# Linear attention and a gated feed-forward block: how the reciprocals of the denominators reach the rows of q

## The chip, the cores and the metric

One Trainium2 chip, one of its cores. The metric is the device time of one execution in microseconds (us); of several executions the median is given. The engines are PE (matrix products, with its weight loads as PEld), DVE, ACT and POOL (elementwise work), and SP, which here only issues transfers. Each runs its own queue in order; sixteen DMA engines move the data.

## The reference

The input x has 2048 rows of 576. It is normalised row by row (xn). Two branches read xn:

```python
qkv = xn @ wqkv                      # 32 heads of 18
phi = lambda t: where(t > 0, t + 1, exp(t)) + 1e-6
pq, pk = phi(q), phi(k)
kv  = einsum("hsd,hse->hde", pk, v)  # one 18 x 18 matrix a head
z   = einsum("hsd->hd", pk)
num = einsum("hqd,hde->hqe", pq, kv)
den = einsum("hqd,hd->hq", pq, z) + 1e-6
s   = (num / den).reshape(S, D) @ wo
g   = silu((gelu(xn @ w_gate) * (xn @ w_up)) @ w_down)
out = x + s * g
```

The change concerns the division by den: one number for each head and each row of x.

## The kernel before, in words

**Layout.** The 2048 rows of x are four blocks of 512 (tb 0 to 3), each of four tiles of 128 (t). Most products run in float32r, each operand cut into a rounded part and a rest (`split`, L101; `halve`, L700), so that a product is a few passes. Products written in plain float32 show as two instructions each in the trace. Nearly every instruction is pinned to the order in which the program writes it (`act`, `vec`, `mm`, `pool`, `dma`, L86 to L99), so the order on each engine's queue is the order of the text; all of these helpers' instructions carry the helper's line (PE L93, DVE L90, ACT L87, POOL L96, transfers L99), and the trace's groups are told apart by tiles.

**The order of the work.** First k and v for the 16 tiles, one `kv_tile` (L475) a tile: three products `x_mm` (c = 0, 1, 2; the third also gives 64 columns of q), the elementwise `k_post`, `v_post`, `q_parts`, `q_post`, and `kv_mm` (L366), which adds to the matrices kv of all heads; the operands of the next tile are made by `place` and `norm`, whose statistics come from `x_next` (L1213, `bn_stats` on DVE). After tile 7 come q's products for blocks 0 and 1 (`q_store`, L512, whose result goes to DRAM), after tile 15 those for blocks 2 and 3 (`q_hold`, L517, whose result stays in SBUF). Between these stand lists of other work, written out by hand (`behind`, `aside`). Then s for all blocks (`s_mm`, L720; 28 products a tile), then 36 matrices of the gate and up products and the down products, which are most of the time and which the diff doesn't touch.

**q.** phi(q) lies with q's columns on the partitions and the rows of x along the free dimension, in five groups (gi): four of seven heads (126 partitions, and on the last two partitions two of the columns of the last head, so that these four are full), and a fifth of four heads (72 columns; `q_turn`, L457, transposes it and two rows for each of the four groups out of the third product of a tile). `phi` (L355) is: a minimum with zero, on ACT (`Relu` of -q) for odd blocks and on DVE for even ones; a maximum on DVE; exp on ACT; an add on POOL.

**kv times wo.** `kv_done` (L562) masks kv's sums into kvm. `kv_wo(gi)` (L588) multiplies a group of kvm by its rows of wo and cuts the result into kvh and kvl, the operands of s. One more column of wo, which is 1 in row 0 only, gives z, the sum of phi(k), as the last column of the second product of each group. From z DVE makes `zc`, z placed in a column a head with the mask `maskh` (part of the tile named small in the trace). `move_rows` (L626) copies the rows of the last head to the last two partitions of the four groups, zc's by way of zx (in the tile named eps_t).

**The division before.** `den(tb)` (L671) multiplies zc by phi(q): 20 small products into one bank, quarters of the block on quarters of the partitions, so that the 32 heads' denominators of 512 rows stand as 128 x 128. DVE adds 1e-6 and takes the reciprocal (tile r); ACT and DVE lay r out as the operand rd (tile aux), rounded part and rest. `scale(tb, gi)` (L692) multiplies `sel`, a matrix of ones and zeros, by rd on PE (tile b, 128 x 512), which repeats each head's reciprocal on that head's 18 partitions, and DVE multiplies phi(q) by it. `halve` then makes the operands of s (tile pq). `make_sel` and `copy_sel` build sel on POOL and ACT. The blocks of s come in the order 2, 3, 0, 1; blocks 0 and 1 of phi(q) are loaded back from DRAM by SP (`q_load`, L526) while s of the blocks before runs.

**Space.** PSUM has six shared banks (`bank`) and two of another ring (`own_bank`). The SBUF slots that matter here are b7 and b8 (a block of phi(q) each; b7 held a fifth of the weights of k and v before), b15 (aux before) and b12 and b14 (wo and kvm, later the operands pq of every second block).

Of the kernel before, what the change touches and what calls it, by code (L numbers as in the profile page):

```python
# [55 lines left out]
def block_kernel(ctx, tc, x, xe, xt_d, wq_d, wkv0_d, wkv1_d, wkv2_d, wo, wgu_d, wd_d, out):  # L56
# [330 lines left out]
    pkv, pks, vas, es, pqt, ph4, ph, ph_d = ({} for _ in range(8))  # L387
# [69 lines left out]
    def q_turn(t):  # L457
# [5 lines left out]
        if i == 0:  # L463
            ph4[tb] = gl_tile([P, TBN], f"ph4_{tb}")
            if tb < 2:
                ph_d[tb] = dr.tile([P, NHG, TBN], F32, name=f"phd_{tb}")
        act(ph4[tb][:, i * P : (i + 2) * P], b[:, 0:P2], AF.Copy)
        if i == 2 and tb < 2:
            dma(out=ph_d[tb][:, 4, :], in_=ph4[tb])
# [5 lines left out]
    def kv_tile(t, early=(), middle=(), end=(), after=()):  # L475
# [7 lines left out]
        if t % 2 == 0 and t % (2 * TT):  # L483
            q_turn(t - 2)
# [5 lines left out]
        run(list(middle))  # L490
        if t - 1 in vas:
            kv_mm(t - 1)
# [6 lines left out]
    def q_mm(tb, gi, o):  # L499
# [10 lines left out]
        phi(o, pq, f"q{tb}_{gi}", tb % 2 == 1)  # L510

    def q_store(tb, gi):  # L512
        o = gl_tile([P, TBN], f"ph_{tb}_{gi}")
        q_mm(tb, gi, o)
        dma(out=ph_d[tb][:, gi, :], in_=o)

# [6 lines left out]
    def ph_of(tb, gi):  # L523
        return ph4[tb] if gi == 4 and tb > 1 else ph[tb][:, gi, :]
# [17 lines left out]
    def make_masks():  # L542
# [15 lines left out]
        band(at["maskh"], ones.rearrange("p (g h) -> p g h", g=NHG), [[-GW, NHG], [DH, H]], 1)  # L558
# [14 lines left out]
    def load_wo():  # L573

        n = NHG * P
        t = big(14, [P, 2 * n + D + 2], F32, "kvm")
        at["one"] = t[0:H, n + D + 2 :].rearrange("p (g j) -> p g j", g=NHG)
        at["kvm"] = t[:, 0:n].rearrange("p (g j) -> p g j", g=NHG)
        at["wo"] = w = big(12, [P, 4, D + 2], F32, "wo_t")
        at["wo4"] = w4 = t[:, n : n + D + 2]  # L580
# [5 lines left out]
        dma(out=w4[1 : W4 + 1, 0:D], in_=wo[4 * GW : D, :])  # L586

    def kv_wo(gi):  # L588
# [8 lines left out]
        zc, mh = at["zc"], at["maskh"]  # L597
# [3 lines left out]
        for c, cs in enumerate((slice(0, HALF), slice(HALF, D + 2))):  # L601
            pw.append(bank(f"kw_{gi}_{c}"))
            mm(
                pw[c][0:wdt, 0 : cs.stop - cs.start], at["kvm"][0:k, gi, 0:wdt], w[0:k, cs],
# [3 lines left out]
        z = pw[1][:, HALF : HALF + 1]  # L608
# [6 lines left out]
        if gi == 4:  # L615
            vec("tensor_copy", zx[x_], z[x_])
# [3 lines left out]
        vec("tensor_scalar", zc[r, gi, :], mh[r, gi, :], z[r], None, op0=ALU.mult)  # L620
# [5 lines left out]
    def move_rows():  # L626
        for gi in range(4):
            r, e = slice(Q4 + 2 * gi, Q4 + 2 * gi + 2), slice(GW, P)
            dma(out=at["zc"][e, gi, H - 1 : H], in_=zx[r])
# [3 lines left out]
    def make_sel():  # L633

        n = NHG * P
        buf = big(15, [P, n + TBN], F32R, "aux")
        at["sel"] = sel = buf[:, 0:n].rearrange("p (g j) -> p g j", g=NHG)
        at["rd"] = rd = buf[:, n : n + TBN]
        one = at["one"]
        pool("memset", one, 1.0)  # L640
        four, last = one[:, 0:4, 0:GW], one[:, 4, :].rearrange("p (r j) -> p r j", r=2)
        for o, pattern, base in ((four, [[GW, 4], [1, GW]], 0), (last, [[0, 2], [1, Q4]], 4 * GW)):
            pool(
                "affine_select",
                out=o, in_=o, compare_op=ALU.is_ge, fill=0.0, base=base,
                pattern=pattern, channel_multiplier=-DH,
            )
            pool(
                "affine_select",
                out=o, in_=o, compare_op=ALU.is_ge, fill=0.0, base=DH - 1 - base,  # L650
                pattern=[[-s_, n_] for s_, n_ in pattern], channel_multiplier=DH,
            )
        pool(
                "affine_select",
            out=one[:, 0:4, GW:P], in_=one[:, 0:4, GW:P], compare_op=ALU.is_ge, fill=0.0,
            base=1 - H, pattern=[[0, 4], [0, P - GW]], channel_multiplier=1,
        )
        pool("memset", rd.bitcast(F32), 0.0)

    def copy_sel():  # L660
        one, sel = at["one"], at["sel"]
        for i in range(4):
            r = slice(i * H, (i + 1) * H)
            if i % 2:
                act(sel[r], one, AF.Copy)
            else:
                pool("tensor_copy", sel[r], one)

    HB = TBN // 4

    def den(tb):  # L671

        pd = bank(f"d_{tb}")
        for gi in range(NHG):
            for i in range(4):
                mm(
                    pd[H * i : H * (i + 1), 0:HB], at["zc"][:, gi, :],
                    ph_of(tb, gi)[:, i * HB : (i + 1) * HB],
                    start=(gi == 0), stop=(gi == NHG - 1),
                )  # L680
        r = gl_tile([P, HB], f"r_{tb}")
        rd = at["rd"]
        vec("tensor_scalar", r, pd[:, 0:HB], EPS, None, op0=ALU.add)
        vec("reciprocal", r, r)
        for i in range(4):
            c, rows, low = slice(i * HB, (i + 1) * HB), slice(H * i, H * (i + 1)), i ^ 1
            act(rd[rows, c], r[rows], AF.Copy)
            vec("tensor_sub", rd[H * low : H * (low + 1), c], r[rows], rd[rows, c].bitcast(F32))

    pqs, s_d, words = {}, {}, {}  # L690

# [743 lines left out]
```

## Time and profile before

| | |
|---|---|
| median of 3 runs | 1492.97 us (1492.86 to 1493.04) |
| the profiled execution | 1492.91 us |
| its span, first to last instruction | 1491.2 us |
| PE / DVE / ACT / POOL busy | 99% / 71% / 38% / 36% of the span |
| granted clock of PE | 1.000 |
| q's products of blocks 2 and 3, with kv times wo | about 183 to 217 us of the span |
| s | about 217 to 286 us |

The times in a row of the trace start at the first instruction of the span. The span is 1.7 us shorter than the execution's own time. A row of the order of time has start, duration, engine, line, operation, output and inputs, shape, count, and in brackets how long the engine was idle before it and who ended that. A row of a group has busy time and mean duration behind the first bar, and the idle time before its instructions with its enders behind the second. A row of a stage lists the busy time of PE, PEld, DVE, ACT and POOL, the granted clock, the share of the DMA engines and their rate.

### The profile page before, as it was taken

What the parts mean: (1) busy time and instruction counts of PE and PEld (TensorE: products, weight loads), DVE (VectorE), ACT (ScalarE), POOL (GpSimd) and SP (SyncE); (2) the same over time, 40 slices, a digit from 0 to 9 for tenths busy, and PEclk for the clock granted to TensorE, in tenths of its full rate; (3) what the DMA queues carried; (4) which work ended last, traced back from release to release, by engine and by line L of the source; (5) the groups of instructions that cost most, each with busy time, mean ns of one, the idle gap of its engine ahead of it and who ended that gap; (6) DMA issues with size and microseconds to landing.
All of it is one profiled execution on the core that took longest, in us unless ns stands there. A gap on an engine that the chain in (4) does not pass through costs nothing.

```text
span 1491.2 us, 22334 instructions
## 1 busy us (share of the span) xinstructions
PE 1481.9 (99%) x8355; PEld 1327.8 (89%) x8355; DVE 1063.9 (71%) x1586; ACT 560.9 (38%) x1043; POOL 543.6 (36%) x521
## 2 busy tenths in 40 slices
PE   9999999999999999999999999999999999999998
PEld 8989989988888888888888888888899999999998
DVE  7667577377788787788787778787785575555775
ACT  5535445332232232332222322223445454445443
POOL 5442431144665544565554565554310020001120
PEclk9999999999999999999999999999999999999999
DMA  6355015533443423444433344333697766686873
GB/s 238 131 213 180 1 43 194 206 149 132 165 173 144 162 106 132 149 174 152 157 119 122 143 173 171 138 134 119 216 335 252 235 215 220 226 292 217 299 253 113
DMA packets 114614, 260.67 MB, mean 175 GB/s; under 512 B 10234, under 2 KB 38778, under 8 KB 112458
## 3 DMA queue, kind: packets, MB, share of 16 engines
q1 hardware_dynamic: 112730, 249.95, 46.7%
q0 software_dynamic: 1632, 8.91, 1.6%
q8 instruction: 65, 1.06, 0.3%
q10 hardware_dynamic: 144, 0.39, 0.1%
q14 instruction: 43, 0.35, 0.1%
HBM read 161.27 MB, written 97.91 MB: 174 GB/s over the span
## 4 chain that ended last, share of the span: by engine, by line
PE 94%; DVE 2%; DMA 2%; ACT 1%; issue 0%; POOL 0%; SPq 0%; ACTq 0%; DVEq 0%; POOLq 0%
PE bd L1010 27%; PE al L804 15%; PE ga L804 15%; PE de L804 15%; PE be L804 8%; PE kv L93 6%; PE s L93 4%; PE q L93 2%; DMA kept_T<-xo_T 1%; PE kv_a L93 1%; ACT xo_T L87 0%; DMA xf_B<-in_xt_dram 0%; PE d L93 0%; PE kw L93 0%; DVE xo_T L90 0%
## 5 line engine op out<-in xcount | busy, mean ns | idle before, releaser
L1010 PEld LDWEIGHTS bd<-t,s 128*128 128x128 f32 x3024 | 400.9, 188 | 0.1
L1010 PE MATMUL bd<-t,s 128*128 128x288 f32 x3024 | 401.0, 295 | 0.0
L90 DVE TENSOR_TENSOR s<-sr,s 128x512 fp32r<-128x512 f32 x252 | 176.1, 739 | 119.8 <-ACT s L87 117.8
L87 ACT ACTIVATE s<-sr 128x512 fp32r<-128x512 f32 x252 | 149.1, 626 | 189.0 <-PE bd L1010 131.0
L96 POOL TENSOR_TENSOR hs<-h,h 128x512 f32<-128x512 f32 x68 | 94.7, 1401 | 203.8 <-DVE h L90 201.1
L87 ACT ACTIVATE h<-h 128x512 f32<-128x512 f32 x108 | 67.1, 633 | 244.5 <-POOL sm L96 123.1
L96 POOL TENSOR_TENSOR sx<-sx 128x288 f32<-128x288 f32 x24 | 27.9, 1180 | 322.9 <-DVE sx L90 321.8
L93 PE MATMUL kv<-wkv,xo_B 128*128 128x416 f32 (+1 forms) x672 | 129.9, 349 | 0.0
L93 PEld LDWEIGHTS kv<-wkv,xo_B 128*128 128x128 f32 x672 | 121.4, 188 | 1.3 <-POOL wkv L96 0.2
L90 DVE TENSOR_TENSOR wa<-raw,wa 128x256 fp32r<-128x256 f32 x72 | 79.2, 1100 | 50.8 <-ACT wa L87 47.5
L96 POOL TENSOR_TENSOR sm<-raw 128x384 f32<-128x384 f32 x72 | 75.8, 1053 | 107.1 <-DMA raw<-in_wgu_dram 86.5
L90 DVE TENSOR_TENSOR h<-h,u 128x512 f32<-128x512 f32 x108 | 95.7, 886 | 3.7
L87 ACT ACTIVATE wa<-sm 128x1152 fp32r<-128x1152 f32 x36 | 41.8, 1161 | 135.8 <-PE de L804 135.8
L90 DVE TENSOR_TENSOR wa<-sm,wa 128x768 fp32r<-128x768 f32 x72 | 63.1, 877 | 36.9 <-ACT wa L87 36.1
L96 POOL TENSOR_TENSOR td<-td 128x288 f32<-128x288 f32 x72 | 70.1, 973 | 53.0 <-DMA td<-in_wd_dram 48.7
L90 DVE TENSOR_TENSOR wb<-raw,wb 128x256 fp32r<-128x256 f32 (+1 forms) x108 | 72.0, 666 | 7.3 <-ACT wb L87 5.8
L90 DVE TENSOR_TENSOR wb<-sm,wb 128x256 fp32r<-128x256 f32 x72 | 61.3, 852 | 20.6 <-ACT wb L87 20.0
L87 ACT ACTIVATE u<-al 128x512 f32<-128x512 f32 x72 | 40.9, 592 | 88.4 <-PE al L804 88.4
L90 DVE TENSOR_TENSOR u<-u,ga 128x512 f32<-128x512 f32 x72 | 49.3, 686 | 19.9 <-PE ga L804 19.3
L804 PE MATMUL al<-xo_B,wa 128*128 128x512 f32 x252 | 63.0, 389 | 0.0
L804 PE MATMUL be<-xo_T,wa 128*128 128x512 f32 x252 | 63.0, 389 | 0.0
L804 PE MATMUL be<-xr_T,wa 128*128 128x512 f32 x252 | 63.0, 389 | 0.0
(175 smaller groups left out, 2773.4 us busy)
## 6 DMA issues: line engine op xcount, KB each, us to landing
sr<-hs SPq DMA_DIRECT2D x252, 256.0 KB
hs<-h SPq DMA_DIRECT2D x68, 512.0 KB
raw<-in_wgu_dram SPq DMA_DIRECT2D x36, 768.0 KB
hs<-hs SPq DMA_DIRECT2D x102, 256.0 KB
td<-in_wd_dram SPq DMA_DIRECT2D x18, 576.0 KB
td<-td SPq DMA_DIRECT2D x18, 576.0 KB
tr<-td SPq DMA_DIRECT2D x16, 576.0 KB
tr<-in_wd_dram SPq DMA_DIRECT2D x12, 576.0 KB
```

The source lines that it names most:

```text
L87: pin(nc.scalar.activation(*args, **kw))
L90: pin(getattr(nc.vector, op)(*args, **kw))
L93: pin(nc.tensor.matmul(*args, **kw))
L96: pin(getattr(nc.gpsimd, op)(*args, **kw))
L804: nc.tensor.matmul(o, w[0:rows, wi, :], xop[0:rows, xi, :], start=(start and n == 0), stop=(n == len(PASSES) - 1), skip_group_check=True,)
L1010: nc.tensor.matmul(banks[j][:, 0:HALF], hw[n, s][:, a, t * P : (t + 1) * P], w[:, c, g % 4], start=(new and g == 0 and m == 0), stop=(g == ...
```

## The change

The products with sel go, with sel, rd and their making. The reciprocals r (32 heads by 512 rows) are written to DRAM (`rd`) by a transfer from POOL's queue, and `to_rows` reads them back by six transfers from POOL's queue into `rb`, which holds for each of q's 128 partitions and five groups the reciprocal of its head. `scale` is now one DVE product of phi(q) and rb, both in SBUF. The first of the six carries four groups. The heads have other numbers inside zc and den: the head in place i of the full group g has the number 4 i + g, and `make_masks` builds maskh accordingly.

- z comes from products of its own, `key_sums`, ahead of `kv_wo`, with the copies to zx and zc and the four small transfers for zc's last rows, which were in `kv_wo` and `move_rows`. kv_wo's second product has 288 columns instead of 290.
- The blocks of s come in the order 0, 2, 3, 1. Block 0 is loaded from DRAM ahead of q's products of block 2; block 3 is stored to DRAM and loaded back. Block 3's denominators are summed in three pieces between other work, by `den_mm`, from the tiles that are stored.
- `phi` takes its minimum on ACT for all blocks.
- `q_turn` stands behind the third product of its tile, and not behind the second.
- `x_next` for tiles 10, 12 and 14 stands earlier in the lists.

```diff
-    def phi(o, src, name, even):
+    def phi(o, src, name):
         e = tmp(list(o.shape), f"e_{name}")
-        if even:
-            act(e, src, AF.Relu, scale=-1.0)
-        else:
-            vec("tensor_scalar", e, src, 0.0, None, op0=ALU.min)
+        act(e, src, AF.Relu, scale=-1.0)
         vec("tensor_scalar", o, src, 0.0, EPS, op0=ALU.max, op1=ALU.add)
-        act(e, e, AF.Exp, scale=-1.0 if even else 1.0)
+        act(e, e, AF.Exp, scale=-1.0)
         pool("tensor_add", o, o, e)
...
         x_mm(t, 1)
-        if t % 2 == 0 and t % (2 * TT):
-            q_turn(t - 2)
...
         x_mm(t, 2)
         run(list(middle))
+        if t % 2 == 0 and t % (2 * TT):
+            q_turn(t - 2)
...
+    def key_sums():
+        pz = bank("z")
+        zc, mh = at["zc"], at["maskh"]
+        for gi in range(NHG):
+            wdt, k = (W4, W4 + 1) if gi == 4 else (GW, GW + 1)
+            w = at["wo4"] if gi == 4 else at["wo"][:, gi]
+            mm(
+                pz[0:wdt, 2 * gi : 2 * gi + 2], at["kvm"][0:k, gi, 0:wdt], w[0:k, D : D + 2],
+                start=True, stop=True,
+            )
+        x_ = slice(Q4, W4)
+        vec("tensor_copy", zx[x_], pz[x_, 8:9])
+        for gi in range(NHG):
+            r = slice(0, Q4 if gi == 4 else GW)
+            z = pz[r, 2 * gi : 2 * gi + 1]
+            vec("tensor_scalar", zc[r, gi, :], mh[r, gi, :], z, None, op0=ALU.mult)
+        for gi in range(4):
+            dma(out=zc[GW:P, gi, H - 1 : H], in_=zx[Q4 + 2 * gi : Q4 + 2 * gi + 2])
...
-    def make_sel():
...
-    def copy_sel():
...
+    def den_mm(tb, gi, src, first, last):
+        if first:
+            dens[tb] = own_bank(f"d_{tb}")
+        for i in range(4):
+            mm(
+                dens[tb][H * i : H * (i + 1), 0:HB], at["zc"][:, gi, :],
+                src[:, i * HB : (i + 1) * HB], start=first, stop=last, skip_group_check=True,
+            )
+
+    def den_end(tb):
+        r = gl_tile([P, HB], f"r_{tb}")
+        vec("tensor_scalar", r, dens[tb][:, 0:HB], EPS, None, op0=ALU.add)
+        vec("reciprocal", r, r)
+        rd[tb] = dr.tile([H, TBN], F32, name=f"rd_{tb}")
+        dma(out=rd[tb].rearrange("h (i c) -> i h c", i=4), in_=r, eng=nc.gpsimd)
...
+    def to_rows(tb):
+        rb[tb] = o = big(15, [P, NHG, TBN], F32, f"rb_{tb}")
+        four = rd[tb][0 : 4 * HG].rearrange("(i g) c -> i (g c)", g=4)
+        dma(
+            out=o[0:GW, 0:4, :].rearrange("p g c -> p (g c)"),
+            in_=four[:, None, :].to_broadcast([HG, DH, 4 * TBN]), eng=nc.gpsimd,
         )
+        last = rd[tb][H - 1 : H, None, :]
+        dma(out=o[GW:P, 0:4, :], in_=last.to_broadcast([2, 4, TBN]), eng=nc.gpsimd)
+        for r in (0, Q4):
+            for h, n, k in ((4 * HG, 3, DH), (H - 1, 1, Q4 - 3 * DH)):
+                src = rd[tb][h : h + n, None, :].to_broadcast([n, k, TBN])
+                dma(out=o[r : r + n * k, 4, :], in_=src, eng=nc.gpsimd)
+                r += n * k
...
     def scale(tb, *gs):
         for gi in gs:
-            pb = bank(f"b_{tb}_{gi}")
-            mm(pb, at["sel"][:, gi, :], at["rd"], start=True, stop=True)
             p = ph_of(tb, gi)
-            vec("tensor_mul", p, p, pb)
+            vec("tensor_mul", p, p, rb[tb][:, gi, :])
...
-    q_hold(2, 7, [
-        [lambda: kv_mm(2 * N0 - 1), kv_done, lambda: difference(1, 3)],
-        [lambda: q_turn(2 * N0 - 2), lambda: kv_wo(4)],
-        [lambda: kv_wo(0), lambda: kv_wo(1), move_rows],
-        [lambda: kv_wo(2), lambda: kv_wo(3)],
+    q_load(0, 7)
+    q_hold(2, 8, [
+        [lambda: kv_mm(2 * N0 - 1), kv_done],
+        [key_sums, lambda: q_turn(2 * N0 - 2), lambda: difference(1, 3)],
+        [lambda: den(0), lambda: to_rows(0), lambda: kv_wo(4)],
+        [move_rows, lambda: kv_wo(0), lambda: kv_wo(1)],
     ])
-    q_hold(3, 8, [
-        [lambda: den(2)],
-        [lambda: scale(2, 0, 1), lambda: halve(2, 0, 1)],
-        [lambda: scale(2, 2, 3), lambda: halve(2, 2, 3)],
-        [lambda: scale(2, 4), lambda: halve(2, 4)],
-    ])
+    behind = [
+        [lambda: kv_wo(2), lambda: scale(0, 0, 1), lambda: halve(0, 0, 1)],
+        [lambda: kv_wo(3), lambda: den(2), lambda: scale(0, 2, 3), lambda: halve(0, 2, 3),
+         lambda: den_mm(3, 4, ph4[3], True, False), lambda: den_mm(3, 0, pg[0], False, False)],
+        [lambda: scale(0, 4), lambda: to_rows(2), lambda: halve(0, 4),
+         lambda: den_mm(3, 1, pg[1], False, False)],
+        [lambda: q_load(3, 7)],
+    ]
+    for gi in range(4):
+        q_store(3, gi)
+        run(behind[gi])
...
     aside = {
...
+        (0, 0): [lambda: den_mm(3, 2, pg[2], False, False), lambda: den_mm(3, 3, pg[3], False, True), lambda: den_end(3),
+                 lambda: build(1, "T1", X_SLOT["T1"])],
+        (0, 1): [lambda: scale(2, *five), lambda: halve(2, *five), lambda: to_rows(3),
+                 lambda: q_load(1, 8)],
+        (0, 3): [lambda: build(1, "T3", X_SLOT["T3"]), lambda: load_mat(0)],
+        (2, 0): [lambda: scale(3, *five), lambda: halve(3, *five), lambda: back("B11")],
+        (2, 1): [lambda: build(1, "T2", X_SLOT["T2"]), lambda: den(1), lambda: to_rows(1)],
+        (2, 3): [lambda: build(1, "T4", X_SLOT["T4"]), lambda: back("T2")],
+        (3, 0): [lambda: mat_sums(0)],
+        (3, 1): [lambda: scale(1, *five), lambda: halve(1, *five)],
+        (3, 3): [lambda: back("T1")],
...
-    for tb in (2, 3, 0, 1):
+    for tb in S_ORDER:
```

More of the change, by code (lines that the diff above doesn't have):

```diff
@@ L386, in block_kernel @@
     left = {}
-    pkv, pks, vas, es, pqt, ph4, ph, ph_d = ({} for _ in range(8))
+    pkv, pks, vas, es, pqt, ph4, ph, ph_d, pg = ({} for _ in range(9))
     def x_mm(t, c, passes=None, new=bank):
@@ L509, in q_mm @@
                 n += 1
-        phi(o, pq, f"q{tb}_{gi}", tb % 2 == 1)
+        phi(o, pq, f"q{tb}_{gi}")
     def q_store(tb, gi):
@@ L523, in ph_of @@
     def ph_of(tb, gi):
-        return ph4[tb] if gi == 4 and tb > 1 else ph[tb][:, gi, :]
+        return ph4[tb] if gi == 4 and tb == 2 else ph[tb][:, gi, :]
     def q_load(tb, i):
@@ L660, in copy_sel @@
-    def copy_sel():
[L661 to L688, printed above, removed]
+    HB = TBN // 4
@@ new lines, in den @@
+    def den(tb):
+        for gi in range(NHG):
+            den_mm(tb, gi, ph_of(tb, gi), gi == 0, gi == NHG - 1)
+        den_end(tb)
+    def to_rows(tb):
[4 more added lines that the diff above has]
+            in_=four[:, None, :].to_broadcast([HG, DH, 4 * TBN]), eng=nc.gpsimd,
+        )
+        last = rd[tb][H - 1 : H, None, :]
[5 more added lines that the diff above has]
+                r += n * k
```

83 lines of the change are left out of this document (25 added, 58 removed).

## The prediction, made before the change was run

> **What bounds the kernel now.** I read the page first (busy shares, slices, chain), then the waits of PE, then a table by stage, then the order of time in the stages that change.
>
> ```profile
> span 1491.2 us, 22334 instructions
> PE 1481.9 (99%) x8355; PEld 1327.8 (89%) x8355; DVE 1063.9 (71%) x1586; ACT 560.9 (38%) x1043; POOL 543.6 (36%) x521
> PEclk9999999999999999999999999999999999999999
> PE 94%; DVE 2%; DMA 2%; ACT 1%; issue 0%; POOL 0%; SPq 0%; ACTq 0%; DVEq 0%; POOLq 0%
> ```
>
> PE works for all but 9.3 us of the span at the full granted clock, and 94% of the chain is PE. So a product that goes saves its own time, unless something else comes late in the place that it leaves.
>
> ```profile
> PE qx L462 <- POOL w_q L96: 1.1, 1, 1.1
> PE b L93 <- DVE aux L90: 0.2, 1, 0.2
> ```
> ```profile
> 183.00:217.40 34.40, 34.40 (x193) 27.80 (x192) 27.25 (x50) 16.71 (x36) 14.41 (x12) 1.00 0.01 3
> 217.40:285.60 68.20, 67.98 (x586) 65.71 (x585) 39.24 (x64) 32.19 (x66) 7.49 (x9) 1.00 0.47 174
> ```
>
> Two of PE's few waits lie in what the diff touches. In the two stages of the change (q's blocks 2 and 3, then s) the columns are PE, PEld, DVE, ACT and POOL: PE has no gap, DVE is 79% and 58% busy, POOL 42% and 11%, and the DMA engines are idle in the first stage. There is room beside PE, but a queue in order can still be late.
>
> **What goes from PE.** The twenty products b (five a block).
>
> ```profile
> 226.10 0.69 PE L93 MATMUL s<-kv,pq 128*128 128x288 f32 x4
> 226.63 0.63 PE L93 MATMUL b<-aux 128*128 128x512 f32 x2
> 227.10 0.42 PE L93 MATMUL s<-kvh,pq 128*128 128x288 f32 x2
> ...
> 230.82 0.85 PE L93 MATMUL b<-aux 128*128 128x512 f32 x3
> 231.51 0.42 PE L93 MATMUL s<-kvh,pq 128*128 128x288 f32 x2
> ```
>
> From start to start two take 0.47 us and three 0.69: 1.16 a block, 4.64 in all. With the wait of 0.2 above: **-4.8 us**.
>
> The turn of q's last columns moves behind the third product of its tile (x_mm(t, 2)).
>
> ```profile
> 132.90 0.27 PE L462 MATMUL qx<-ident,w_q 128*128 128x128 f32 x1
> 134.22 0.33 PE L462 MATMUL qx<-ident,w_q 128*128 128x128 f32 x1 [1.05 <-POOL w_q L96]
> 134.31 2.72 PE L93 MATMUL kv<-wkv,xo_B 128*128 128x384 f32 x14
> ```
>
> The wait of 1.05 us for POOL falls inside the 2.6 us of those 14 products: **-1.05**. DVE's shift of x_next by a tile leaves the operands of tile 10 as late as now, with over a microsecond to spare by my count; I cost that at nothing (0 to +1 if the spare is gone).
>
> **What comes to PE.** key_sums: five products in fp32 with two columns, ten instructions in the trace's counting (all fp32 products show twice). None such is shown; the nearest rows:
>
> ```profile
> 186.37 1.04 PE L93 MATMUL kv_a<-pk,va 128*127 128x126 f32 x8
> 187.25 0.29 PE L93 MATMUL kv_b<-pk,va 128*73 128x72 f32 x2
> 187.35 1.41 PE L93 MATMUL q<-xo_B,wq 128*128 128x512 f32 x5
> ```
>
> 0.11 us an instruction with 126 columns, 0.05 with 72: 0.5 to 1.1 us, I take **+0.8**. The sums of denominators (160 instructions) stay, but block 3's are cut into three groups, and a return from fp32 to the other form costs.
>
> ```profile
> 239.12 1.23 PE d L93 x40
> 240.35 3.91 PE s L93 x28
> 244.26 0.47 PE b L93 x2
> 244.73 3.72 PE s L93 x28
> ```
>
> 28 products take 3.91 us behind d and 3.72 behind b. I count seven fp32 groups before and eight after, since kw and den now share some: **+0.2**. So PE's own work and known waits: -4.85.
>
> **What now waits.** T is microseconds from q's first product of block 2 (183.06 in before). With 3.3 for 14 products of q, 1.0 for kv_mm, 0.9 for a kv_wo, 1.3 for a den, PE reaches den(0) at T 12.0, s of block 0 at 36.6, the last denominators of block 3 at 40.8.
>
> *First wait: den(0) on the two rows that SP copies into zc.*
>
> ```profile
> 192.64 0.16 DVE L90 COPY eps_t<-kw 8x1 f32<-8x1 f32 x1
> ```
> ```profile
> 192.83 0.71 SPq L99 DMA_DIRECT2D small<-eps_t  x1
> 193.70 0.62 SPq L99 DMA_DIRECT2D kvh<-kv  x1
> 194.41 0.56 SPq L99 DMA_DIRECT2D kvl<-kv  x1
> ```
> ```profile
> GB/s 0 0 0 0 0 0 0 0 0 0 0 18 0 0 18 0 0 0 0 18 0 18 0 0 0 0 18 0 0 18 0 33 0 0 0 18 0 0 18 0
> ```
>
> Before, den came 5 us behind these transfers. Now DVE copies the sums when phi's max of q's second product is done, T 9.3; SP issues four transfers 0.6 apart from there (0.03 after the copy, as above). The last row is the DMA rate from 192 to 202 in quarters: the 4.5 KB of kvh, issued at 193.70, move at 194.75. Landing at 1.1 (these bytes) to 3.5 us (the shortest landing listed, 512 KB below); I take 1.7: they land at T 11.0 to 12.9, and the group that needs the last is multiplied at 12.9. **+0.3** (0 to 2). Behind it stands PE's whole queue.
>
> *Second wait: POOL.* It issues the write of the reciprocals, waits until that has landed, issues six transfers, and only then does what stands behind.
>
> ```profile
> 215.35 1.30 POOL L96 TENSOR_TENSOR ph<-ph,e_q 128x512 f32<-128x512 f32 x1 [2.35 <-DVE ph L90]
> ```
> ```profile
> 1090.15 1.08 POOL L99 DMA_DIRECT2D hs<-hs  x2
> ```
> ```profile
> 239.99 0.70 POOL L99 DMA_DIRECT2D xr_B<-kept_B  x1 [19.72 <-ACT s L87]
> ```
> ```profile
> xr_T<-kept_T POOLq DMA_DIRECT2D x3, 1280.0 KB, 7.2
> hs<-h POOLq DMA_DIRECT2D x4, 512.0 KB, 3.5
> xr_B<-kept_B POOLq DMA_DIRECT2D x1, 1280.0 KB, 9.3
> ```
>
> An issue is 0.54 us (0.70 at most), so six are 3.2, and 1280 KB, just what the rows of a block weigh, land in 7.2 to 9.3 us. A broadcast from DRAM is not in the trace; I take 7.2, its own smaller rows included. Block 0: den ends at T 13.6, reciprocal (0.95) and sum 15.0, write landed 18.1, rows landed 25.3. DVE wants them behind phi and kv_wo(2), at 25.5: just hidden. Behind the waiting POOL stand the memset for kv4 and phi's add for q's fourth product; den(2) needs that one only at 27.9, and it is done by 24.
>
> Block 2 is the tight one. DVE's queue from 25.5 holds, without a gap, scale and halve of block 0, phi's max of three products and the second reciprocal:
>
> ```profile
> 214.51 0.69 DVE L90 TENSOR_SCALAR ph<-q 128x512 f32<-128x512 f32 x1 [0.24 <-ACT e_q L87]
> 215.12 1.28 DVE L90 TENSOR_TENSOR ph<-ph,b 128x512 f32<-128x512 f32 x2
> 216.50 1.30 DVE L90 TENSOR_TENSOR pq<-ph,pq 128x512 fp32r<-128x512 f32 x2
> ```
>
> At 0.6 to 0.7 each it frees rb at T 35.5. POOL then issues six (3.2) and adds q's last phi (1.3): 40.0 to 41. PE needs that add at 40.8: **+0.5** (0 to 2).
>
> A row shows how the add can be longer:
>
> ```profile
> 174.70 0.72 POOL L96 TENSOR_TENSOR w_q<-w_q 128x64 f32<-128x64 f32 x2 [0.80 <-ACT w_q L87]
> ...
> 183.48 3.52 POOL L96 TENSOR_TENSOR w_q<-w_q 128x64 f32<-128x64 f32 x2 [1.07 <-ACT w_q L87]
> ```
> ```profile
> 183.27 3.55 DVE L90 TENSOR_TENSOR xf_B<-xf_B,xf_B 128x1536 f32<-128x1536 f32 x2
> ```
>
> The same two adds took 3.52 us instead of 0.72 beside a DVE operation with both inputs in SBUF. Scale's second factor now lies in SBUF, so this can happen beside it too; one such product is 0.6 us and is inside the bound of 2. The Trainium skill ("SBUF — State Buffer", Who interferes with whom) says the same, that such an operation and a GpSimd read lock each other out for a whole instruction; by it the second wait would be nearer 1.1 than 0.5, and the trace agrees with the lock.
>
> *The rest is hidden.* Blocks 2, 3 and 1 have 12, 16 and 11 us from POOL's first issue to the first s that needs them, against 7.2 and some 4 us of DVE. SP's loads of q's blocks wait for their slots and hold the stores of s behind them; tmp has four buffers for those. What DVE and ACT no longer do (four subtractions and copies a den, DVE's min for even blocks) is off the path.
>
> **Sum.** -4.8 - 1.05 + 0.8 + 0.2 + 0.3 + 0.5 = -4.05 from the profiled execution's 1492.91 us (span 1491.2 and 1.7 around it), which is 0.06 under the median 1492.97: **1488.9 us**.
>
> **Rivals.**
>
> *The stalls eat the gain.* With issues of 0.70 (six: +1.0), rows in 9.3 us (block 0 lands at 27.4, 1.9 later than DVE wants, and DVE's gapless queue hands that on to rb and to the last add), and key_sums at 1.1, the sum is +3 more: 1491.9, no difference that shows. For it: POOL's queue and DVE's are in order and have under a microsecond to spare. Against: 0.54 and 7.2 are the usual rows.
>
> *Slower: rows from DRAM come much later than a plain load.* The place is scale of block 0. From a landing of some 8 us after the first issue each microsecond more is one of PE's at the last denominators of block 3, and from 12 block 2 adds as much again, since s of block 2 starts at T 53 and POOL's issue for it at 36. At 16 us the cost is 8 + 4: 1501. It decides from about 14 on (8 - 2 make up the 4 gained and 3 above). For it: 18 rows read the same 8 KB each, in a shape no row shows. Against: nothing else uses the DMA engines in the first stage (3 GB/s), and 1280 KB in 16 us would be 80 GB/s where the loads shown make 140 to 180.
>
> The Trainium skill ("DMA: Bandwidth & Descriptors", Rules for kernel authors) has a rule against the change: an outermost dimension under 16 confines a transfer to that many engines. The broadcast's source goes out as 7 regions, and seven sixteenths of that page's 341 GB/s make an estimate of 6.9 us for the moving of the big transfer, so a landing near 8.5 and a sum near 1490. No run here shows it yet.
>
> *The change does not do what it says:* the products go but PE is held elsewhere by as much. With no gap in PE and room on DVE I see no such place beyond the two waits above; it is within the first rival.
>
> **Chances.** A measurement of this kernel tells 0.2%, 3.0 us, from no change. My forecast with its bounds (1486.9 to 1490.2): 0.62; better still: 0.04; first rival, to 1493: 0.20; slower by transfers: 0.14. That makes faster 0.68 (a fifth of the first rival and most of the forecast), same 0.17, slower 0.15. The range 1486.9 to 1493.0 leaves out the last case and the better one.
>
> **What would show it.** Right: no b on PE; the wait of qx gone; PE's waits name small's transfer before the first d, and ph's add by POOL before the third group of block 3's d, each under a microsecond; the rows land about 7 us behind the issue. Wrong: PE waiting on DVE for pq at the start of s, six issues of POOL far above 3.2 us, a DVE wait on rb, or a wait that moves to the first gate products. The sum is wrong if key_sums takes more than 1.1 us or PE's pitch changes beside the transfers.

## The result: 18 us slower

The changed kernel takes 1511.09 us (median; 1507.97 to 1512.7) where the kernel before takes 1492.97: ratio **1.0118**, 95% interval 1.0103 to 1.0133. The forecast was 1488.9. The profiled execution took 1509.51 us, with a span of 1507.8, so 16.6 us more span than before. Of the executions behind the ratios in this text two took far longer than the rest (5462.67 us of e9, 2649.49 us of the kernel before) and are left out of the ratios.

The page of the changed kernel: span, busy shares, granted clock in 40 slices, and the chain.

```profile
span 1507.8 us, 22351 instructions
PE 1483.9 (98%) x8345; PEld 1328.6 (88%) x8345; DVE 1055.3 (70%) x1562; ACT 558.4 (37%) x1033; POOL 560.2 (37%) x549
PEclk9999998999999999999999999999999999999999
PE 89%; DVE 3%; DMA 3%; issue 3%; POOL 1%; ACT 1%; SPq 0%; POOLq 0%; ACTq 0%; DVEq 0%
```

PE is busy 2 us more than before although the products b are gone, the chain's PE share fell from 94% to 89%, and the clock row shows an 8 in the seventh slice (226 to 264 us), which the row of before doesn't have. So the loss has a place. PE's waits name it (microseconds in all, times, longest):

```profile
PE d L93 <- DMA ph<-phd: 9.4, 1, 9.4
PE s L93 <- ACT pq L87: 2.9, 1, 2.9
PE d L93 <- POOL ph L96: 2.4, 1, 2.4
...
PE s L93 <- DVE pq L90: 1.0, 1, 1.0
```

Four new waits, 15.8 us. The largest is den(1), the denominators of block 1, waiting for SP's load of that block (ph from phd). The next one in size is the first s of block 1, waiting for pq, which waits for rows (the 1.0 belongs to it); the third is the last denominators of block 3, waiting for POOL's add of phi. None stands at scale of block 0.

The same waits in order of time, PE's rows:

```profile
226.34 0.43 PE L93 MATMUL d<-ph,small 128*32 128x128 f32 x8 [2.44 <-POOL ph L96]
...
255.05 2.36 PE L93 MATMUL d<-ph,small 128*32 128x128 f32 x40 [9.44 <-DMA ph<-phd]
...
261.82 0.42 PE L93 MATMUL s<-kvh,pq 128*128 128x288 f32 x2
...
283.56 0.85 PE L93 MATMUL s<-kvh,pq 128*128 128x288 f32 x2 [2.92 <-ACT pq L87]
...
285.91 1.33 PE L93 MATMUL s<-kvh,pq 128*128 128x288 f32 x4 [1.02 <-DVE pq L90]
...
290.83 0.42 PE L93 MATMUL s<-kvh,pq 128*128 128x288 f32 x2
...
294.56 0.42 PE L93 MATMUL s<-kvh,pq 128*128 128x288 f32 x2
```

The forty products d behind the long wait take 2.36 us, against 1.23 in the prediction's row of before. A table by stretches says why; the column behind the five engines is the granted clock.

```profile
250.00:255.00 5.00, 0.00 (x0) 0.00 (x0) 0.00 (x0) 0.00 (x0) 0.00 (x0) 0.50 1.01 276
255.00:259.00 4.00, 3.95 (x47) 3.60 (x48) 2.17 (x4) 1.45 (x3) 0.00 (x0) 0.52 0.77 278
259.00:263.00 4.00, 4.00 (x32) 4.00 (x31) 2.58 (x5) 2.52 (x6) 0.00 (x0) 1.00 0.34 140
283.50:289.80 6.30, 5.22 (x21) 4.87 (x22) 4.85 (x8) 3.62 (x9) 0.57 (x1) 0.52 0.32 126
```

**A long wait of PE is paid twice.** The clock falls to 0.50 while PE stands idle, and stays at about 0.5 for the next 4 to 6 us. The tile of s behind den(1) is done 6.77 us after that den began (255.05 to 261.82), where the prediction's rows of before have 5.14 from 239.12 to 244.26: 1.6 us. The first tile of block 1 takes 7.27 us (283.56 to 290.83) and the next 3.73 (to 294.56); take off the wait of 1.02 and 2.5 remain. So 15.8 of waits and 4.1 of half clock, less the gain of 3.6 that the first experiment below measures, make 16.3 of the 16.6 us.

What holds the load? First the rows of reciprocals alone, block 0, 200 to 212 us: the DMA engines' busy share in forty slices (tenths), what was moved, and landing times from the issue.

```profile
DMA  1010000670544545757888765764663499510001
...
DMA packets 919, 1.66 MB, mean 138 GB/s; under 512 B 566, under 2 KB 566, under 8 KB 790
...
rb<-rd POOLq DMA_DIRECT2D x1, 1008.0 KB, 9.9
```

Though almost nothing else is moving, the share is 0.4 to 0.8, not 0.9, and the transfer needs 9.9 us; the prediction took 7.2 from a plain load. Then the stretch of the long wait, 232 to 260 us, in which block 3's rows, the loads of q's blocks and the transfer of B11 back meet:

```profile
DMA packets 2024, 7.17 MB, mean 256 GB/s; under 512 B 701, under 2 KB 701, under 8 KB 1548
...
xr_B<-kept_B POOLq DMA_DIRECT2D x1, 1280.0 KB, 20.9
rb<-rd POOLq DMA_DIRECT2D x1, 1008.0 KB, 19.8
```

What POOL's queue has in flight takes about 20 us. Block 1's load is issued into that:

```profile
233.54 0.32 SPq L99 DMA_DIRECT2D ph<-phd  x1
...
238.84 0.32 SPq L99 DMA_DIRECT2D ph<-phd  x1
```

The second of these is block 1's, and den(1) begins at 255.05: 16.2 us from the issue. PE had come to it at 245.61 (255.05 less 9.44), 6.8 us from the issue. In the kernel before the same pair stands far apart. Block 1 is the last block of s in both orders, but den(1) stood behind the first tile of the third block, and now stands behind the second tile of the second, so that its rows have time to come:

```profile
236.99 0.40 SPq L99 DMA_DIRECT2D ph<-phd  x1
```
```profile
256.52 1.30 PE L93 MATMUL d<-ph,small 128*32 128x128 f32 x40
```

That is 19.5 us, more than the 16.2 here and the 18.6 that e2 shows below. The change takes 12.7 us of this cover away and puts new transfers into what is left. DVE waits for rows in the same way, for the first block little, for blocks 3 and 1 long:

```profile
211.17 1.29 DVE L90 TENSOR_TENSOR ph<-ph,rb 128x512 f32<-128x512 f32 x2 [2.84 <-DMA rb<-rd]
...
256.83 2.50 DVE L90 TENSOR_TENSOR ph<-ph,rb 128x512 f32<-128x512 f32 x4 [14.68 <-DMA rb<-rd]
...
282.15 3.10 DVE L90 TENSOR_TENSOR ph<-ph,rb 128x512 f32<-128x512 f32 x5 [12.45 <-DMA rb<-rd]
```

**Theory A:** the rows' transfers are the cause through their *shape*. One broadcast whose outermost dimension is seven loads only some of the DMA engines, is slow itself, and holds back a plain load beside it, which ends when its slowest share ends. **Rivals:** B, it is the *bytes*: the 1280 KB more a block (1008, two of 108, two of 20 and one of 16) would do the same as one plain load. C, it is only the *dependence*: scale can't run before the rows, and DVE's queue does the rest. D, it is *another transfer*: B11 back, or the order of SP's loads.

### The profile page after: what moved, and what is told of

Its sections match the earlier page's. It is cut to its first block, busy times and chain, and to the rows that moved or that the text cites. A ratio compares the mean times of both kernels' runs of the same rounds, so it can differ in the third digit from the quotient of the medians.

```text
span 1507.8 us, 22351 instructions
## 1 busy us (share of the span) xinstructions
PE 1483.9 (98%) x8345; PEld 1328.6 (88%) x8345; DVE 1055.3 (70%) x1562; ACT 558.4 (37%) x1033; POOL 560.2 (37%) x549
## 4 chain that ended last, share of the span: by engine, by line
PE 89%; DVE 3%; DMA 3%; issue 3%; POOL 1%; ACT 1%; SPq 0%; POOLq 0%; ACTq 0%; DVEq 0%
PE bd L1012 26%; PE al L806 15%; PE ga L806 15%; PE de L806 15%; PE be L806 8%; PE kv L93 6%; PE s L93 2%; DMA rb<-rd 1%; PE kv_a L93 1%; DMA kept_T<-xo_T 1%; DVE xf_B L90 0%; DVE ph L90 0%; PE q L93 0%; DMA xf_B<-in_xt_dram 0%; DVE xo_T L90 0%
## 5 line engine op out<-in xcount | busy, mean ns | idle before, releaser
L806 PE MATMUL al<-xr_B,wa 128*128 128x512 f32 x252 | 63.0, 389 | 0.0
```

The costliest lines, as they stand in the source:

```text
L806: nc.tensor.matmul(o, w[0:rows, wi, :], xop[0:rows, xi, :], start=(start and n == 0), stop=(n == len(PASSES) - 1), skip_group_check=True,)
```

## The experiments

All edits are to the changed kernel unless another is named. Times are medians; each ratio, with its 95% interval in brackets, stands to runs of the kernel before on the same chip. A trace is of one execution.

**e1: no rows at all.** Neither r's write to DRAM nor the six transfers; scale multiplies by a constant tile, so the division by the denominators is left out.

```
-        rd[tb] = dr.tile(...); dma(out=rd[tb]..., in_=r, eng=nc.gpsimd)
...
-        (the six transfers of to_rows)
+        pass
...
-            vec("tensor_mul", p, p, rb[tb][:, gi, :])
+            vec("tensor_mul", p, p, half[:, None, :].to_broadcast(...))
```

> The kernel after without the seven transfers of the reciprocals (the write and the six): scale multiplies by a constant tile, so the division is left out. This measures what is left of the change when no rows move. My sum for PE's own work (products b out, key sums and one group in, the turn moved) was -4.85 us: 1488.1, and at most 0.5 more for the small transfers to zc. If it is above 1492, another part of the change (order of the blocks, loading block 3 back, DVE's min moved to ACT) costs by itself. If the late load of block 1 (9.4 us of waiting in the profile after) is due to the rows' traffic, that wait is gone here; if it is due to its slot and its place in SP's queue, several us of it stay and the time is near 1495.

1489.67 us, ratio 0.9979 [0.9969, 0.9989]. All four waits are gone. So everything lost comes through the rows, and the rest of the change gains 3.6 us (1.6 to 4.6 by the interval).

**e2: rows moved, not read.** All seven transfers stay; scale reads e1's constant (division left out again).

> The kernel after with all seven transfers, but scale multiplies by a constant tile, so nothing waits for the rows (the division is left out). Theory 'traffic': the rows' transfers load the DMA engines, block 1's load stays late, PE still waits some 3 to 9 us there and the time is 1494 to 1502. Theory 'dependence': what costs is that DVE waits for the rows and with it everything behind in its queue; then this run is within 2 us of the run without transfers.

1501.74 us, 1.0055 [1.004, 1.007]. PE's rows have one large wait left:

```profile
252.66 2.36 PE L93 MATMUL d<-ph,small 128*32 128x128 f32 x40 [8.51 <-DMA ph<-phd]
```
```profile
234.01 0.32 SPq L99 DMA_DIRECT2D ph<-phd  x1
```

The second row is the issue of block 1's load in the same run: 18.6 us to den(1). The traffic alone, without any reader, costs 12 us over e1; C can explain the other 9 at most.

**e3: the broadcast in two halves.** Two transfers of 504 KB, two groups of heads each, in the same order otherwise. It adds one issue of POOL a block.

```
-            out=o[0:GW, 0:4, :]..., in_=four[:, None, :].to_broadcast([HG, DH, 4 * TBN])
+        for c in range(0, 4, 2):
+            out=o[0:GW, c : c + 2, :]..., in_=four[:, None, c * TBN : (c + 2) * TBN].to_broadcast([HG, DH, 2 * TBN])
```

> The kernel after with the big broadcast of each block cut in two transfers of 504 KB (groups 0 and 1, groups 2 and 3), so seven issues of POOL and not six. In the profile after, the DMA engines are 0.4 to 0.5 busy while only block 0's rows move, as if seven of sixteen worked. Theory 'seven engines': two transfers go to different sevens, the rows land in 6 to 7 us and not 9.9, everything behind is earlier, and the time falls to 1492 to 1500. Rival 'volume': the same bytes and one more issue: 1508 to 1513.

1503.07 us, 1.0069 [1.0054, 1.0084]: 8 us better than the changed kernel with the same bytes. Waits of 3.9 (block 1's load), 3.6 and 1.6 (pq), 1.3 (POOL) are left.

**e4: B11 back later**, from (2, 0) to (3, 0).

> The kernel after with one transfer moved: the load back of B11 (1280 KB, POOL's queue) stands behind the first tile of s of block 3 and no longer behind the first of block 2, where it runs beside block 1's load. Theory 'volume': some 1.3 MB less in the 24 us in which 7.2 MB moved, so block 1's load lands 3 to 5 us earlier: 1504 to 1507. Theory 'seven engines': the slowest seven engines are held by the rows of block 3 that were issued before it, and B11 stands behind them in the same queue: within 2 us of after.

1510.69 us, 1.0117 [1.0101, 1.0132]. The wait for the load fell from 9.4 to 6.4, and the time didn't follow. About 1.7 us of what was saved went elsewhere: in this trace the clock fell behind the 2.4 us wait for POOL too (last section). B11 back is at most 3 us of the 9.4, so D's first half is not the cause.

**e5: block 1's load ahead of block 3's**, into a slot that is free earlier (T3 is built earlier for that, and B11 and T1 change places).

```
-        [lambda: q_load(3, 7)],
+        [lambda: build(1, "T3", X_SLOT["T3"]), lambda: q_load(1, 13), lambda: q_load(3, 7)],
```

> The kernel after with one load moved: T3's operand is built a little earlier, so that its slot b13 takes block 1 of q, whose load is then issued behind q's last product and ahead of block 3's load and of block 3's rows (B11 goes to b8 and T1 to b13 instead). The transfers of the rows are unchanged. Theory 'traffic': block 1's load is no longer beside block 3's rows when PE needs it, so the wait of 9.4 us, the later wait for block 1's rows and the half clock behind them (about 17 us together) go, less some 2 to 5 us that stay because block 3's load and rows are later by as much as block 1's load takes: 1494 to 1499. Rival: block 3's load takes its place as the late one: above 1503.

1511.51 us, 1.0123 [1.0107, 1.014]. The wait for the load is gone; 5.5 us for ACT's copies of s at the first tile of block 3, and 6.4 for pq at the first of block 1 (2.9 before this edit), stand in its place; DVE still waits 14.6 us for block 3's rows. The order of SP's loads moves the loss and doesn't remove it: D's second half isn't the cause either.

**e6: e2 and e3 together**: halves, not read (division left out).

> The run in which nothing waits for the rows, with the big broadcast in two halves; the division is left out (scale multiplies by a constant tile). The same with one big transfer was 1501.7, without any rows 1489.7. Theory 'seven engines': what made block 1's load late was seven of sixteen engines loaded with the rows; with two halves on different engines most of the 12 us go: 1490 to 1495. Rival 'volume': the bytes are the same, so 1499 to 1503.

1494.85 us, 1.0013 [1.0004, 1.0022]. Against e2's 1501.74, the same bytes and no reader: 6.9 us by the cut alone. The wait for block 1's load is 3.0.

**e7: the same weight as one plain load.** The six transfers are replaced by one load of 1280 KB, a region for each partition, out of q's own storage. Scale waits for it and reads it as it would the rows; the values aren't the reciprocals, so the division is left out.

```
-        (the six transfers of to_rows)
+        dma(out=o, in_=ph_d[0], eng=nc.gpsimd)
```

> The kernel after with the six transfers of a block replaced by one plain load of 1280 KB over 128 partitions (from the DRAM copy of q's block 0, into which the reciprocals are written first, so that it waits for that write as the rows do); the values are not the reciprocals, so the division is wrong. The same bytes, one issue of POOL, 128 rows of 10 KB. Theory 'shape' (seven engines, small pieces, six issues): it lands in 5 to 7 us, and the time is 1490 to 1495. Rival 'volume': block 1's load is still late: 1500 or more.

1490.72 us, 0.9982 [0.9972, 0.9991]: no slower than before, with as many bytes and with the dependence, and 1 us above e1. A wait of 1.3 for block 1's load is left. **B and C fall** as causes by themselves: bytes and a dependence on rows that come in time cost about 1 us together. (The dependence on rows that come late stays a part of the loss, at most the 9 us between e2 and the changed kernel.) The DMA answer of 232 to 260 us, to be set beside that of the changed kernel above:

```profile
DMA packets 1961, 8.81 MB, mean 315 GB/s; under 512 B 240, under 2 KB 240, under 8 KB 1421
...
rb<-phd POOLq DMA_DIRECT2D x2, 1280.0 KB, 8.6
...
xr_B<-kept_B POOLq DMA_DIRECT2D x1, 1280.0 KB, 10.5
```

More is moved in the same stretch, 315 GB/s instead of 256, and the neighbour xr_B lands in 10.5 us, not 20.9. Alone (200 to 212 us) the plain load keeps the DMA engines at nine tenths and lands in 6.0:

```profile
DMA  0005000000291949997998950100000000000398
...
rb<-phd POOLq DMA_DIRECT2D x1, 1280.0 KB, 6.0
```

e7 changes three things at once (how many engines, six issues to one, hardly any small packets). That the first matters is shown by e3 and e6, whose edit works the other way on the other two: one issue more, and pieces of 4 KB in place of 8.

The single pieces, counted in the kept traces, show the engines more directly than the shares. While block 0's rows move alone, seven pieces of 8 KB are in flight at a time, 14 of 4 KB with the halves (e3), and 16 of 10 KB with the plain load (e7). Block 1's load has 128 pieces. In the changed kernel the first starts at 241.03 and the last ends at 253.57, 12.5 us; in the kernel before it is 4.3, in e3 8.4, in e7 7.2. Half of the 128 are there in 5.2 us, and the last 16 alone need 3.9: the load does wait for a slow share. The records don't name the engine of a piece, so that this share is the one on the broadcast's seven engines is inferred. A second cost of the shape stays open: a 4 KB piece of the halves takes about 0.3 us and an 8 KB piece of the one broadcast 0.35, so the halves land only 2.4 us sooner with twice the engines. What the small pieces cost was not measured by itself.

**e8: halves, and the work spread**: e3's halves, e5's early load, block 3's last denominators one step later at (0, 1), other places for load_mat and for B11 and T2 back.

> A version meant to beat both: two halves, block 1 loaded early into b13, block 3's last denominators one tile later (so POOL's six issues for block 2 are no longer ahead of an add that PE waits for), and the loads of the first gate matrix and of B11 behind the second block of s. If the traffic beside q's loads and the place of the add are the whole cost, it comes near the run without rows: 1489.5 to 1492. If the rows cost in another way as well, it stays above 1495.

1501.43 us, 1.0051 [1.0034, 1.0068]. Only the start of block 1's s is late now (4.1 and 1.8 for pq). DVE's rows show the reason:

```profile
249.87 3.10 DVE L90 TENSOR_TENSOR ph<-ph,rb 128x512 f32<-128x512 f32 x5 [12.53 <-DMA rb<-rd]
...
258.40 0.95 DVE L90 RECIPROCAL r<-r 128x128 f32<-128x128 f32 x1
```

The reciprocal of block 1 stands in DVE's queue behind the scale of block 3, which waits for its rows; so block 1's rows start late.

**e9: e8 with den(1) ahead of scale(3)**; only to_rows(1), which needs the buffer, stays behind it.

```
-        (2, 0): [scale(3, *five), halve(3, *five)],
-        (2, 1): [build T2, den(1), to_rows(1)],
+        (2, 0): [den(1), scale(3, *five), halve(3, *five)],
+        (2, 1): [build T2, to_rows(1)],
```

> On top of the spread version (two halves, block 1's load before block 3's, the sums of block 3 one step later; 1501.43 us, with waits of 4.1 and 1.8 us at the first s of block 1): the sums of block 1, their reciprocal and its write to DRAM now stand ahead of the scale of block 3, so that VectorE doesn't hold them behind the rows of block 3; only the six transfers stay behind it. Theory (what is left in the spread version is the order of VectorE's work, which makes block 1's rows late): the wait for pq at the first s of block 1 goes, and with it the half clock behind it; 1490 to 1493 us. Rival (the landing of the rows itself is too long between the blocks, because one buffer holds the rows of all blocks and the next six transfers can't start before the last scale has read it): a wait of 2 to 5 us stays there, 1497 to 1501 us.

> e9 once more, for a profiled execution that is not disturbed, and beside e12 on the same chip. Theory: 1490.5 to 1492.5 us, no wait of PE for ph or pq over 1 us, and the first s of block 1 at the granted clock 1.00. Rival: a wait of 1 to 2 us at the first s of block 1 is left.

1492.35 us, 0.9988 [0.9979, 0.9997], and measured again 1492.18, 0.9993 [0.9983, 1.0002]. All of PE's waits of the second measurement but those of the first 10 us:

```profile
PE s L93 <- ACT s L87: 0.6, 1, 0.6
PE xt L213 <- DVE x L90: 0.3, 1, 0.3
```

Every wait for rows or loads is gone, and with it the half clock. Nothing of the work is left out here: this is the change with its rows from DRAM, 19 us faster than as it was made, and level with the kernel before.

**e10: e9's order with the one broadcast.**

> The same order as in e9, but with one broadcast transfer for four groups of heads, as in the changed kernel. It tells how much of the cure is the order and how much the shape of the transfer. Theory (both are needed, since the one broadcast holds its seven engines some 10 us alone and nearly 20 us beside the loads): 4 to 8 us slower than e9, with a wait of PE for ph or pq between 225 and 290 us. Rival (the order alone cures it): within 1 us of e9.

1498.14 us, 1.0032 [1.002, 1.0045]: 5.8 us slower than e9, as expected, though not by the waits that were expected: block 1's load is in time, and PE waits for ACT's s and a little for pq.

```profile
PE s L93 <- ACT s L87: 2.3, 1, 2.3
...
PE s L93 <- DVE pq L90: 0.6, 2, 0.4
```

Behind the first of them the granted clock fell, to a mean of 0.91 in these 20 us:

```profile
250.00:270.00 20.00, 17.72 (x121) 17.36 (x120) 12.51 (x18) 10.92 (x21) 4.04 (x7) 0.91 0.63 204
```

2.9 of waits, where e9 has 0.6, and 1.8 of clock (0.09 of 20 us) are 4.1 of the 5.8. The order alone (all that e5, e8 and e9 move, together) cures 13 of the 19 us and the cut alone (e3) 8; both are needed for all of it.

**e11: the kernel before, with the moved turn alone.**

```
         x_mm(t, 1)
-        if t % 2 == 0 and t % (2 * TT):
-            q_turn(t - 2)
...
         run(list(middle))
+        if t % 2 == 0 and t % (2 * TT):
+            q_turn(t - 2)
```

> The kernel before, with one part of the change alone: the turn of q's last heads stands behind the third product of x instead of ahead of it. Theory of the prediction (three waits of PE for POOL's w_q, 1.05 us in all, go and nothing takes their place): 1491.9 us, ratio 0.9993. Rival (the waits were cover for something that is late next, such as VectorE's kv operand, as the wait for xo_B in the changed kernel suggests): 1492.7 to 1493.3 us, no change.

1495.81 us, 1.0015 [1.0007, 1.0024]: 2.4 us *slower*. The waits for w_q are gone, and PE waits for other operands instead:

```profile
PE kv L93 <- DVE xo_B L90: 1.6, 2, 1.0
PE mr L194 <- DVE mv L90: 1.0, 1, 1.0
```

These are 1.5 us more than the 1.1 that went. This execution was the slowest of eleven, and 1.3 us of what it lost were lost by 25 us, ahead of the first turn; so the rows explain the loss in part.

**e12: e9 with the turn where it was before.**

> e9 with one part of the change undone: the turn of q's last heads stands ahead of the third product of x again, as in the kernel before. Theory of the prediction (the moved turn is worth the 1.05 us of three waits for POOL's w_q): 1 us slower than e9, some 1492.8 us. Rival (alone in the kernel before, the moved turn cost 2.4 us: it shifts VectorE's and ACT's work, and waits for xo_B and mv take the place of those for w_q; in the changed kernel only the moved x_next mends this): as fast as e9 or faster, 1489 to 1491.5 us.

1491.15 us, 0.9986 [0.9978, 0.9995], no slower than e9 although 0.7 us of the wait for w_q is back. The moved turn is worth nothing in the changed kernel either. This is the lowest median of a version that leaves nothing out, about 2 us under the kernel before; the 1.0 us between it and e9 is within the intervals.

## Why the prediction was wrong, step by step

- **Products b gone, -4.8; key_sums +0.8; one more fp32 group +0.2.** Right. e1 measures a gain of 3.6 for all that isn't rows; these three and the first wait below sum to 3.5. key_sums has a place of its own in PE's rows, ten instructions as forecast and 0.93 us from its start to that of the next product, at 191.15:

```profile
190.22 0.94 PE L93 MATMUL z<-wo_t,kvm 127*126 127x2 f32 x8
191.02 0.27 PE L93 MATMUL z<-kvm 73*72 73x2 f32 x2
```

- **The turn, -1.05.** Wrong, by e11 and e12. The prediction counted the wait that went and costed the operands of the next tiles at nothing; in e11 those are the next late thing (1.6 + 1.0 us). The changed kernel has neither wait, and no gain from the turn either (e12); that the moved x_next keeps those operands in time there is likely but not shown, since no run moved it alone. A wait of an engine with no slack behind it is not a gain until the next operand has been timed.
- **First wait, den(0) on zc, +0.3.** Right, though the list of PE's waits doesn't name it, since it stands inside a row of forty products. The row, and the weight loads of its last two groups of heads:

```profile
194.69 1.58 PE L93 MATMUL d<-ph,small 128*32 128x128 f32 x40
```
```profile
195.59 0.41 PEld L93 LDWEIGHTS d<-ph,small 128*32 128x32 f32 x16 [0.31 <-DVE xf_B L90]
```

  The forty take 1.58 us instead of 1.30, and the fourth group comes at T 12.95 (195.59 from 182.64; forecast 12.9). The view names DVE's xf_B, which den doesn't read; the last bytes of SP's fourth transfer moved at 195.20, and PE went on 0.3 to 0.4 behind them. That this transfer is the releaser is inferred.
- **Second wait, POOL's add, +0.5 (0 to 2).** Right place and reason, size wrong: 2.44. POOL's rows:

```profile
219.97 1.60 POOL L96 TENSOR_TENSOR ph<-ph,e_q 128x512 f32<-128x512 f32 x1 [2.21 <-ACT e_q L87]
221.52 3.47 POOL L99 DMA_DIRECT2D rb<-rd  x6
225.00 1.28 POOL L96 TENSOR_TENSOR ph<-ph,e_q 128x512 f32<-128x512 f32 x1
```
```profile
219.74 0.68 DVE L90 TENSOR_TENSOR ph<-ph,rb 128x512 f32<-128x512 f32 x1
```

  Six issues (3.47; forecast 3.2) and an add (1.28; forecast 1.3) are as counted. They began at 221.52 and not at the 218 that the prediction has (T 35.5 from 182.64). The term that was mis-sized is the landing of block 0's rows, 9.9 us instead of 7.2: DVE's scale began 2.84 late (211.17, above) and worked on almost without a gap until it freed rb; ACT's copies for pq wait for that scale, and the exponential for which POOL's add waits stands behind them. The rival's rate, one microsecond of PE for each of landing beyond 8, gives 1.9 more than 0.5, and 2.44 was measured. Other landings go with it: 7.5 in e3 with a wait of 1.3, 6.0 in e7 with none. The add ahead of the issues took 1.60 us beside the last of scale (DVE's row), 0.3 more than the add at 225.00, which has no such neighbour. That agrees in kind with the lock between DVE and POOL for which the prediction named the Trainium skill ("SBUF — State Buffer", Who interferes with whom), in another add than the one feared; so it is partly luck that 0.5 and 1.9 meet 2.44 so closely.
- **"The rest is hidden."** This is the step that failed, and most of the loss is here. It set one landing time, 7.2 us from a plain load, against the 11 to 16 us that blocks 2, 3 and 1 have, and said of SP's loads only that they wait for their slots. Block 0's rows took 9.9 us with the DMA engines nearly to themselves, block 3's 19.8 beside the loads, and block 1's load 16.2. The prediction counted the cover of the rows but not that of the load that den(1) needs, which the new order cuts from 19.5 to 6.8 us, and not the traffic that it runs into: 7.17 MB in 28 us. It saw only the average of the stage (0.47 DMA share over 68 us).
- **The half clock.** Not foreseen: 4.1 us, a fifth of the loss.
- **The rival "rows from DRAM come much later than a plain load"** had the direction and the cause, with a chance of 0.14, but not the size (1501 at a landing of 16 us, 8 of the 18 us), and its place is the smaller part. (At 14 us its own rates give 6 + 2 = 8, which covers the 4 gained and the 3 above; the 8 - 2 written there does not.) Scale of block 0, 2.84 us late, gave PE the 2.44 us wait and no more. The rest is lost at block 1, along the chain load, den, reciprocal, write, issues, rows, scale.
- **The rule of the Trainium skill** ("DMA: Bandwidth & Descriptors", Rules for kernel authors), that an outermost dimension under 16 confines a transfer to that many engines, agrees with the runs: seven pieces in flight and a share of 0.4 to 0.8 for a transfer of seven regions beside small ones, 16 and 0.9 for one of 128, and 7 to 8 us gained by cutting it in two. The prediction weighed it for the transfer's own time (a landing near 8.5; 9.9 measured) and not for what the same engines owe to a neighbour, which was the larger part (e2).

What would have shown it beforehand: a list, in order of time, of all transfers that the change issues or moves between 220 and 285 us, each with its first use before and after. The pair 236.99 and 256.52 is in the trace of before.

## What to carry to other kernels

A broadcast or gather whose outermost dimension is small should be costed twice, by its own landing and by what it does to full-width loads in flight beside it; cutting it into pieces that can run on different engines is a cheap test (8 us here for one more issue a block). When an in-order queue must wait for a transfer, put everything that doesn't need it ahead of the wait: one line's move of den(1) took 9 us from 1501 to 1492. And a wait that goes is a gain only if the next operand is already there; time that one before counting.

## What the runs showed of the hardware

- PE's clock: a wait of 9.44 us left the clock at 0.52 for the next 4 us; one of 2.92 us, with another of 1.02 behind it, at 0.52 for 6.3 us. The 2.44 us wait at 226 us left it at 1.00 (first row, the changed kernel), but in e4 the same wait, 2.35 us, was followed by 3.4 us of work at 0.50 (second row).

```profile
226.00:248.00 22.00, 19.27 (x148) 18.84 (x148) 11.11 (x16) 7.16 (x14) 5.07 (x9) 1.00 0.81 227
```
```profile
228.30:231.70 3.40, 3.40 (x17) 3.40 (x16) 2.15 (x3) 0.00 (x0) 0.75 (x1) 0.50 0.60 206
```

  What differs is where the wait falls. In every kept trace but e9's first, the moments at which the granted clock changes lie whole multiples of 3.41 us apart: in the changed kernel 248.6, 258.8, 282.7 and 289.5 are 3, 7 and 2 such steps. PE was idle for 2.0 us of the step that ended as e4's clock fell, for 2.3 in e10 (a wait of 2.28), and for 1.6 at most of any step around 226 us in the changed kernel. How much it takes no run measures: at the start of e7 and e10, between other work, 1.5 us was enough. As far as these traces go, then, one wait costs 1.7 us more or nothing by its place on that grid, and a difference of 1 to 2 us between two traces can be that alone. The Trainium skill ("TensorE: Matmul & The Clock Gate", Part 1: The HAM clock gate) gives an idle window of about 3.4 us that is free-running; the grid agrees with it, and the waits of 2.92, 2.35 and 2.28 show that a shorter idle time can be enough.
- A plain load of 1280 KB that moves in some 5 us alone took 16.2 (changed kernel) and 18.6 us (e2) from its issue to its first use beside a broadcast of seven regions. Alone is block 0's load in the kernel before, issued at 217.86 (first row); the second is the DMA engines' share from 216 to 226 us in quarters, in which its pieces move from 218.9 to 222.9:

```profile
217.86 0.37 SPq L99 DMA_DIRECT2D ph<-phd  x1
```
```profile
DMA  0400000000092298799899899911199700000000
```
